# Fewer word conversions per expert, and another order of the early rows and the second early weight piece

## The chip, the cores and the metric

The kernel runs on one core of one Trainium2 chip. The metric is the device time of one execution in microseconds (us); the time of a kernel is the median of its runs. Matrix products run on TensorE (PE in the profile, its weight loads PEld), elementwise work on VectorE (DVE) and ScalarE (ACT), conversions' additions and all gathers on GpSimd (POOL), most loads are issued by SyncE (SP).

## What is computed

Three stages, one after the other. Inputs and output are float32, but for the last stage's weights: they come as float64, and the chip makes float32 of their high and low words.

```python
# 1: linear attention, 4 x 8 heads, 768 steps, head size 48
for t in range(S):
    state = alpha[:, :, t, :, None] * state + einsum('bhd,bhe->bhde', k[:, :, t], v[:, :, t])
    y[:, :, t] = einsum('bhd,bhde->bhe', q[:, :, t], state)
# 2: mixture of 8 experts over 3072 rows of 384, one expert a row (argmax of the gate's logits)
for e in range(E):
    mask = e_idx == e
    h = np.maximum(x[mask] @ w1[e], 0.0)            # 384 -> 1024
    out[mask] = gate_w[mask, None] * eom[mask, e, None] * (h @ w2[e])   # 1024 -> 384
# 3: a = x @ w1; b = x @ w2; h = a * b @ w3; return h @ w_out
```

## The kernel before

Every large product is made of three TensorE matmuls (`mm3`, lines 168 to 171): each operand is kept as a high part (rounded) and a low part (the rest), and high x high, high x low and low x high are added up in one PSUM bank.

**Attention** goes over 24 blocks of 128 rows (loop over j from line 554). In a step, TensorE makes block j's output (`a_y`), the small gate product of block j + 1 (`a_vw`), the transposed keys (`a_tk`), and the score products of block j + 2 (`a_pt`), which VectorE and ScalarE mask in the next step (`a_mask`). VectorE's queue begins a step with that mask, so what stands behind it (logits, routing, splits) waits when the score products are late. In the last steps the first expert is prepared: the most frequent expert so far is chosen, its first 256 rows are gathered (`k_rows`, two gathers of 128), and `k_turn` (steps 21 and 22) transposes them on TensorE once they have landed; `k_split` makes their low part.

**The first expert** starts with those 256 rows: `k_up(q)` (line 617) multiplies weight piece q of four (two of the eight 128-wide output blocks each) in 18 matmuls of 256 columns. The order written out is: `k_up(0)`, the end of the routing, the gather of the other 208 rows, the feeding of pieces 1 to 3, `k_up(1)`, `early_h(0)`, `k_up(2)`, `early_h(1)`, the transposes of the other rows (`x_turn`), `k_up(3)`, the splits of those rows, then eight passes of nine matmuls over the other rows in three PSUM banks in turn. A piece is fed (`feed`, line 151) by a ScalarE copy that rounds it to the high part and a VectorE difference that gives the low part. The next experts' gathers (`x_gather`) are issued on GpSimd as soon as the row numbers are there.

**Experts** follow one after the other: eight steps of the first projection (`e_up`), eight of the second (`e_down`). Between the steps stand feeds of coming pieces and, from expert 2 on, single steps of a generator (`conv`): the conversion of the last stage's weights. A conversion (`words` and `m_convert`) has four steps: ScalarE's absolute value of the high words (line 132); three VectorE operations (134 to 136); nothing; ScalarE's copy of the low words (139), the load of the next but one (953), GpSimd's addition (141) and a store to DRAM (957). There are 23; three empty steps come first. Its two buffers mean that the first step of conversion c waits for the store of conversion c - 2. All of it stands in the engines' queues between the experts' own evictions (`h_split`: ScalarE's relu and VectorE's low part).

In experts 2, 3 and 4 a step of the generator follows each of the 16 steps, so four conversions an expert; in 5 and 6 one follows each second step of the first projection and every step of the second, so three. After expert 6, `w_prime` multiplies the last two weight matrices (eight blocks f of eight g), with three steps in each block, at g = 1, 4, 7. Expert 7 has none; its second projection is done in three parts d of eight, and each part is stored and split for the last stage.

**Loads.** SyncE loads units of two pieces, 768 KB (`load_ahead`, line 108), in a fixed order: experts 0 to 6 (units 0 to 27), the converted pieces of the first eight units (28 to 35), expert 7 (36 to 39), the other converted pieces (40 to 43). Up to four units are loaded ahead between units 6 and 41, else two. A converted unit must have been stored before its load is issued.

**The last stage** goes over six groups of 512 rows: eight steps of two products (pab) and an elementwise product, then four output tiles of 24 matmuls (o).

Of the kernel before, what the change touches and what calls it, by code (L numbers as in the profile page):

```python
# [23 lines left out]
E = 8  # L24
F = 1024
KF = F // 128
# [30 lines left out]
def attention_then_moe_kernel(ctx, tc, pk0, pka, pkb, wbd_d, wexp, wmlp, cst_d, out):  # L57
# [41 lines left out]
    units = [u for e in range(E - 1) for u in sunits(e)] + runits(0, N_WO + N_W3)  # L99
    units += sunits(E - 1) + runits(N_WO + N_W3, N_D)  # L100
    Y_FIRST, Y_END = 6, len(units) - (N_M + 1) // 2
    assert Y_END % 4 == 0
    stream = [(u, c, key) for u, un in enumerate(units) for c, key in enumerate(un[2])]
    wmlp_w = wmlp.bitcast(I32)
# [1 line left out]
    loaded, freed, fed, pools = [0], [0], [0], {}  # L106

    def load_ahead():
        while loaded[0] < min(freed[0] + (4 if Y_FIRST <= loaded[0] < Y_END + 2 else pools["keep"]), pools["upto"]):
            kind, i, parts = units[loaded[0]]  # L110
            slot = loaded[0] % 4
            if Y_FIRST <= loaded[0] < Y_END and slot > 1:
                raw = ys_p.tile([128, 2 * NPC], I32, tag=f"y{slot - 2}", name="raw")
            else:
                raw = pools["raw"].tile([128, 2 * NPC], I32, tag=pools["tag"], name="raw")
            if 2 <= loaded[0] < 4:
                G.memset(raw[:, 0:1], 0)
            if kind == "r":
                for h in range(len(parts)):
                    SP.dma_start(out=raw.bitcast(F32)[:, h * NPC:(h + 1) * NPC], in_=wm_d[i + h])  # L120
            else:
                SP.dma_start(out=raw.bitcast(F32),
                             in_=wexp[bass.ds(first[i // 4] + i % 4, 1)].rearrange("o p n -> p (o n)"))
            raws[loaded[0]] = raw
            loaded[0] += 1
# [67 lines left out]
    def tiles(n):  # L193
        return [(i, min(128, n - 128 * i)) for i in range((n + 127) // 128)]
# [360 lines left out]
    for j in range(NJ):  # L555
# [47 lines left out]
            A.activation(out=early[4], in_=ps_c[:, 1, :], func=ACTF.Copy)  # L603
        if j == JK + 3:
            k_load()
        if NJ - 3 <= j < NJ - 1:
            k_turn(j - NJ + 3)
        a_pt(j + 2)
        a_dv(j)
        a_next(j - 2)  # L610
        a_alpha(j + 4)
# [2 lines left out]
    ps_k = atp.enter_context(tc.tile_pool(name="ps_k", bufs=4, space=PSUM, reuse_waits="tile"))  # L614
    uk = {}

    def k_up(q):
        w = pieces["e", 0, q]
        uk[q] = ps_k.tile([128, 2, NK], F32, tag="k", name="uk")
        for f in range(2):  # L620
            for k in range(KD):
                sl = slice((f * KD + k) * 128, (f * KD + k + 1) * 128)
                mm3(uk[q][:, f], w[:, 0, sl], w[:, 1, sl], xt[0][:, 0, k, 0:NK], xt[0][:, 1, k, 0:NK], k == 0, k == KD - 1)

    r_expert(*R_LAST)
    r_sort(JK, R_LAST[0])
# [234 lines left out]
            h_tile(2 * q + f)  # L861
            h_split(2 * q + f, uk[q][:, f], 0, NK)

    k_up(1)
    early_h(0)
    k_up(2)
    early_h(1)
    for i, n in tiles(width(0))[2:]:
        for d in range(KD):
            x_turn(bank[d], xg[0], d, i, n, NK)  # L870
    k_up(3)
    for d in range(KD):
        x_split(0, d, xg[0], bank[d])
    interleave(picks())
# [161 lines left out]
    def w_prime():  # L1036
        wpr = wpr_p.tile([128, KF, DM], F32, tag="wpr", name="wpr")
        for f in range(KF):
            ps = ps_u.tile([128, CMX], F32, tag="u", name="u")[:, 0:DM]
            for g in range(KF):  # L1040
# [9 lines left out]
                if f == KF - 1 and g % 2:  # L1050
                    pieces.pop(("o", g // 2))
                    feed(1)
                if g in (1, 4, 7):
                    next(conv, None)
            A.activation(out=wpr[:, f], in_=ps, func=ACTF.Copy)
        pieces.pop(("3", N_W3 - 1))
# [15 lines left out]
    for e in range(E):  # L1072
        if e == 1:
            interleave(windows())
        for f in range(KF if e else 0):
            e_up(e, f, pieces["e", e, f // 2])
            if f % 2:
                pieces.pop(("e", e, f // 2))
            if (f % 2 if e < E - 1 else 3 <= f < 7):
                feed(1)  # L1080
            if e < 5 or e < E - 1 and f % 2 == 0:
                next(conv, None)
        if e == E - 1:
            col = off_of(e)
            for d in range(KD):
                feed((2, 2, 0)[d])
                for f in range(KF):
                    e_down(e, f, pieces["e", e, 4 + f // 2], [d])
                e_store(e, col, [d])
                y_split(0, [d])  # L1090
            for f in range(4):
                pieces.pop(("e", e, 4 + f))
            break
# [163 lines left out]
```

## Time and profile before

| what | us |
|---|---|
| median of 3 timed runs (lowest, highest) | 715.21 (714.85, 718.95) |
| profiled execution, device time | 710.39 |
| its span, first to last instruction | 708.4 |
| TensorE busy in the span | 670.9 |
| TensorE's mean granted clock, share of full | 0.988 |

The span is what the trace covers; the device time has 2 us more around it. By TensorE's matmuls the stages lie as follows: attention to 128.3, the first rows of expert 0 to 139.6, its other rows to 149.6, its second projection from 153.1, expert 1 to 203, experts 2 to 6 to 342, the product of the last weights to 375.4, expert 7 to 401.7, the last stage to 698. In the rows below, "idle before" in square brackets is the time in which the engine stood idle before the instruction, with what ended it; x is a count.

### The profile page before, as it was taken

Reading aid. Unit: us, or ns where it says so; the run is one execution under the profiler, and the core shown is the slowest. Engines: PE = TensorE matmul, PEld = TensorE weight load, DVE = VectorE, ACT = ScalarE, POOL = GpSimd, SP = SyncE. Lnnn points to the kernel's source line nnn. Section 1 sums busy time; section 2 is a strip of 40 time slices with the busy share of each in tenths; the row PEclk is TensorE's granted clock in tenths of the full one; section 3 lists DMA queues with packets and bytes.
Section 4 is the critical chain, followed back from the end, with each engine's and each line's share of the span. In section 5 each row is a group of like instructions: output and inputs, shape, how many; then the busy total and the mean of one; then the engine's idle time right before and its main releaser. Section 6 shows DMA issues by size and latency. Waiting matters only on the chain.

```text
span 708.4 us, 14637 instructions
## 1 busy us (share of the span) xinstructions
PE 670.9 (95%) x5904; PEld 608.3 (86%) x5904; DVE 400.2 (56%) x746; ACT 340.0 (48%) x676; POOL 204.7 (29%) x231
## 2 busy tenths in 40 slices
PE   6999998879999999999999999999999999999993
PEld 3878877769999999999998989989889889889893
DVE  7989998856948899877667464132131230330320
ACT  4787777434446767666656453232232232232220
POOL 2977776230223554452351000101101002001001
PEclk9999999989999999999999999999999999999998
DMA  9999986345267899887894200000000001001000
GB/s 290 244 278 252 248 258 219 132 133 223 90 187 261 312 331 330 298 293 283 282 317 164 90 0 12 34 0 24 23 0 34 12 0 45 1 0 45 1 11 33
DMA packets 28326, 102.53 MB, mean 145 GB/s; under 512 B 4736, under 2 KB 5120, under 8 KB 28256
## 3 DMA queue, kind: packets, MB, share of 16 engines
q1 hardware_dynamic: 21360, 77.26, 33.9%
q0 software_dynamic: 6752, 24.12, 9.8%
q8 instruction: 47, 0.77, 0.5%
q14 instruction: 23, 0.19, 0.1%
q10 hardware_dynamic: 144, 0.20, 0.1%
HBM read 83.07 MB, written 18.48 MB: 143 GB/s over the span
## 4 chain that ended last, share of the span: by engine, by line
PE 60%; DMA 4%; DVE 2%; ACT 2%; issue 1%; POOL 0%; POOLq 0%; ACTq 0%; SPq 0%; DVEq 0%
PE pab L170 9%; PE pab L169 9%; PE pab L171 9%; PE o L170 5%; PE o L169 5%; PE o L171 5%; PE u L169 3%; PE u L170 3%; PE u L171 3%; PE d L170 3%; PE d L169 3%; PE d L171 3%; DMA mraw<-in_wmlp_dram 2%; DMA wm_d<-cva 2%; DVE w L160 1%
## 5 line engine op out<-in xcount | busy, mean ns | idle before, releaser
L1150 DVE TENSOR_TENSOR p_s<-pab,a_s 128x512 f32<-128x512 f32 x48 | 33.2, 692 | 162.7 <-PE pab L171 160.4
L170 PE MATMUL pab<-y,w 128*128 128x512 f32 x288 | 112.0, 389 | 0.0
L169 PE MATMUL pab<-y,w 128*128 128x512 f32 x288 | 112.0, 389 | 0.0
L171 PE MATMUL pab<-y,w 128*128 128x512 f32 x288 | 112.0, 389 | 0.0
L1164 POOL DMA_INDIRECT out_dram<-o_s,idx_o x24 | 23.4, 975 | 296.1 <-ACT o_s L1163 291.7
L160 DVE TENSOR_TENSOR w<-raw,w 128x768 fp32r<-128x768 f32 x87 | 98.5, 1140 | 16.1 <-ACT w L159 14.4
L1152 ACT ACTIVATE ab<-p_s 128x512 fp32r<-128x512 f32 x48 | 30.3, 632 | 102.0 <-DVE p_s L1150 102.0
L159 ACT ACTIVATE w<-raw 128x768 fp32r<-128x768 f32 x87 | 71.9, 840 | 12.9 <-PE d L171 9.5
L169 PE MATMUL d<-h,w 128*128 128x464 f32 (+7 forms) x192 | 69.1, 360 | 3.1 <-ACT w L159 3.1
L141 POOL TENSOR_TENSOR cva<-cva,cvc 128x768 int32<-128x768 int32 x23 | 46.5, 2023 | 85.9 <-ACT cvc L139 70.0
L171 PE MATMUL d<-h,w 128*128 128x464 f32 (+7 forms) x192 | 67.2, 350 | 0.0
L170 PE MATMUL d<-h,w 128*128 128x464 f32 (+7 forms) x192 | 67.1, 350 | 0.0
L169 PE MATMUL o<-wpp,ab 128*128 128x384 f32 x192 | 64.2, 334 | 0.0
L171 PE MATMUL o<-wpp,ab 128*128 128x384 f32 x192 | 64.2, 334 | 0.0
L170 PE MATMUL o<-wpp,ab 128*128 128x384 f32 x192 | 64.2, 334 | 0.0
L171 PEld LDWEIGHTS pab<-y,w 128*128 128x128 f32 x288 | 54.1, 188 | 11.2
L169 PEld LDWEIGHTS pab<-y,w 128*128 128x128 f32 x288 | 54.1, 188 | 11.0
L170 PEld LDWEIGHTS pab<-y,w 128*128 128x128 f32 x288 | 54.1, 188 | 11.0
L169 PE MATMUL u<-xt,w 128*128 128x448 f32 (+6 forms) x168 | 58.5, 348 | 1.8 <-DVE h L851 1.4
L171 PE MATMUL u<-xt,w 128*128 128x448 f32 (+6 forms) x168 | 57.8, 344 | 1.4 <-DVE w L160 1.4
L170 PE MATMUL u<-xt,w 128*128 128x448 f32 (+6 forms) x168 | 57.9, 345 | 0.0
L1153 DVE TENSOR_TENSOR ab<-p_s,ab 128x512 fp32r<-128x512 f32 x48 | 33.2, 692 | 33.5 <-ACT ab L1152 33.5
(243 smaller groups left out, 1479.9 us busy)
## 6 DMA issues: line engine op xcount, KB each, us to landing
raw<-in_wexp_dram SPq DMA_DIRECT2D x32, 768.0 KB, 5.5
mraw<-in_wmlp_dram SPq DMA_DIRECT2D x23, 768.0 KB, 6.2
pb<-in_pkb_dram SPq DMA_DIRECT2D x24, 384.0 KB, 4.8
wm_d<-cva POOLq DMA_DIRECT2D x23, 384.0 KB, 3.7
raw<-wm_d SPq DMA_DIRECT2D x23, 384.0 KB, 4.7
pa<-in_pka_dram SPq DMA_DIRECT2D x42, 192.0 KB, 5.0
x_d<-xs POOLq DMA_DIRECT2D x23, 192.0 KB, 6.4
pa<-in_pka_dram SPq DMA_DIRECT2D x42, 97.5 KB, 5.4
```

Source lines behind the costliest of these rows:

```text
L141: G.tensor_tensor(out=a, in0=a, in1=c, op=ALU.add)
L159: A.activation(out=hl[:, 0], in_=src, func=ACTF.Copy)
L160: low = lambda: eng.tensor_tensor(out=hl[:, 1], in0=src, in1=hl[:, 0], op=ALU.subtract)
L169: T.matmul(out=ps, lhsT=sh, rhs=mh, start=start, stop=False)
L170: T.matmul(out=ps, lhsT=sh, rhs=ml, start=False, stop=False)
L171: T.matmul(out=ps, lhsT=sl, rhs=mh, start=False, stop=stop)
L1150: V.tensor_tensor(out=p_s, in0=pss[1], in1=a_s, op=ALU.mult)
L1152: A.activation(out=t[:, 0], in_=p_s, func=ACTF.Copy)
L1153: V.tensor_tensor(out=t[:, 1], in0=p_s, in1=t[:, 0], op=ALU.subtract)
L1164: G.indirect_dma_start(out=out[:, :], out_offset=bass.IndirectOffsetOnAxis(ap=idx_o[:, n:n + 1], axis=0), in_=o, in_offset=None)
```

## The change

In `load_ahead`, units 32 to 35 (converted pieces) come two ahead in place of four. In the attention loop, `a_pt(j + 2)` stands ahead of `k_turn`. `k_up` can do half a piece (`fs`) and can put all six matmuls with the low weights behind the twelve with the high ones (`low_last`); piece 1 is done so, and piece 3 is halved around the transposes of the other rows. In `w_prime` the first three blocks have four steps of the generator (odd g), the others three, the last none. In the experts, a step follows each second step of the first projection from expert 2 on, expert 7 too; expert 7's second projection has a step after each second f (until the conversions are through), and its feeds of the last stage's pieces are two, none, two in place of two, two, none.

```diff
+    N_LATE = Y_END - 8
...
-        while loaded[0] < min(freed[0] + (4 if Y_FIRST <= loaded[0] < Y_END + 2 else pools["keep"]), pools["upto"]):
+        while loaded[0] < min(freed[0] + (4 if Y_FIRST <= loaded[0] < N_LATE or Y_END - 4 <= loaded[0] < Y_END + 2 else pools["keep"]), pools["upto"]):
...
+        a_pt(j + 2)
         if NJ - 3 <= j < NJ - 1:
             k_turn(j - NJ + 3)
-        a_pt(j + 2)
...
-    def k_up(q):
+    def k_up(q, fs=range(2), low_last=False):
         w = pieces["e", 0, q]
-        uk[q] = ps_k.tile([128, 2, NK], F32, tag="k", name="uk")
-        for f in range(2):
-            for k in range(KD):
-                sl = slice((f * KD + k) * 128, (f * KD + k + 1) * 128)
-                mm3(uk[q][:, f], w[:, 0, sl], w[:, 1, sl], xt[0][:, 0, k, 0:NK], xt[0][:, 1, k, 0:NK], k == 0, k == KD - 1)
+        if fs[0] == 0:
+            uk[q] = ps_k.tile([128, 2, NK], F32, tag="k", name="uk")
+        blocks = [(f, k, slice((f * KD + k) * 128, (f * KD + k + 1) * 128)) for f in fs for k in range(KD)]
+        for part in ((0, 1), (2,)) if low_last else ((0, 1, 2),):
+            for f, k, sl in blocks:
+                for i in part:
+                    T.matmul(out=uk[q][:, f], lhsT=w[:, i // 2, sl], rhs=xt[0][:, i % 2, k, 0:NK],
+                             start=k == 0 and i == 0 and not (low_last and f),
+                             stop=k == KD - 1 and i == 2 and (f == 1 or not low_last))
...
-    k_up(1)
+    k_up(1, low_last=True)
     early_h(0)
     k_up(2)
     early_h(1)
+    k_up(3, [0])
     for i, n in tiles(width(0))[2:]:
         for d in range(KD):
             x_turn(bank[d], xg[0], d, i, n, NK)
-    k_up(3)
+    k_up(3, [1])
...
-                if g in (1, 4, 7):
+                if g % 2 if f < 3 else f < KF - 1 and g in (1, 4, 7):
                     next(conv, None)
...
-            if e < 5 or e < E - 1 and f % 2 == 0:
+            if e < 2 or f % 2 == 0:
                 next(conv, None)
...
-                feed((2, 2, 0)[d])
+                feed((2, 0, 2)[d])
                 for f in range(KF):
                     e_down(e, f, pieces["e", e, 4 + f // 2], [d])
+                    if f % 2:
+                        next(conv, None)
```

## Rows read from the trace of the kernel before

**Rows 1.** Page, span and busy time of TensorE.
```profile
span 708.4 us, 14637 instructions
...
PE 670.9 (95%) x5904; PEld 608.3 (86%) x5904; DVE 400.2 (56%) x746; ACT 340.0 (48%) x676; POOL 204.7 (29%) x231
```

**Rows 2.** Stages: stretch, length; busy PE, PEld, DVE, ACT, POOL; PEclk, DMA share, GB/s.
```profile
139.60:153.10 13.50, 8.77 (x75) 8.34 (x73) 5.39 (x21) 3.72 (x11) 7.61 (x8) 0.86 0.51 152
...
207.60:342.00 134.40, 133.21 (x754) 130.51 (x753) 112.80 (x148) 89.82 (x143) 57.63 (x47) 1.00 0.86 299
342.00:375.40 33.40, 33.40 (x194) 33.20 (x193) 20.27 (x25) 20.86 (x31) 15.11 (x12) 1.00 0.85 295
375.40:401.70 26.30, 24.57 (x147) 23.95 (x147) 18.60 (x24) 15.28 (x26) 2.64 (x2) 1.00 0.39 135
401.70:698.00 296.30, 295.70 (x1440) 261.73 (x1438) 83.73 (x124) 87.64 (x149) 22.42 (x23) 1.00 0.04 16
```

**Rows 3.** Waits of TensorE and its weight loads: us in total, times, longest.
```profile
PE u L171 <- DVE w L160: 1.4, 1, 1.4
PE u L169 <- DVE h L851: 1.4, 3, 0.5
...
PE uk L171 <- DVE w L160: 1.1, 1, 1.1
...
PE ps_c L479 <- DMA xg<-x_d,idx_c: 0.9, 1, 0.9
...
PEld ones L828 <- DMA xg<-x_d,idx_c: 0.3, 1, 0.3
```

**Rows 4.** Timeline of the attention's end: start, length, instruction, idle before and releaser.
```profile
121.80 0.69 DVE L337 TENSOR_TENSOR px<-pts,cm 128x512 f32<-128x512 f32 x1 [1.22 <-PE pts L331]
...
124.33 0.43 ACT L427 ACTIVATE rhs<-ohh,cst 128x160 bf16<-128x160 bf16 x1 [0.55 <-DVE ohh L425]
...
124.97 0.44 PE L365 MATMUL y<-U,q 64*64 64x64 f32 x13 [0.85 <-ACT pb L321]
```

**Rows 5.** Timeline of the early pieces, 131 to 140.
```profile
131.58 2.68 DVE L160 TENSOR_TENSOR w<-raw,w 128x768 fp32r<-128x768 f32 x3
132.58 0.38 PE L171 MATMUL uk<-xt,w 128*128 128x256 f32 x1 [1.07 <-DVE w L160]
...
139.64 0.26 PE L169 MATMUL ones<-xt,w 128*128 128x208 f32 x1
```

**Rows 6.** Timeline of expert 0's other rows and the gathers, 140 to 154.
```profile
140.53 0.97 POOL L201 DMA_INDIRECT xg<-x_d,idx_c  x1 [5.33 <-DVE idx_c L753]
...
149.33 0.95 POOL L201 DMA_INDIRECT xg<-x_d,idx_c  x1 [0.30 <-issue]
...
147.68 0.34 ACT L850 ACTIVATE h<-ps_c 128x208 fp32r<-128x208 f32 x1 [3.25 <-PE ones L171]
151.93 0.34 ACT L850 ACTIVATE h<-pts 128x208 fp32r<-128x208 f32 x1 [3.90 <-remote]
...
153.06 0.75 PE L169 MATMUL d<-h,w 128*128 128x464 f32 x1 [3.06 <-ACT w L159]
```

**Rows 7.** Conversions, 207 to 380: groups by line (busy, mean ns, idle before); DMA issues.
```profile
L141 POOL TENSOR_TENSOR cva<-cva,cvc 128x768 int32<-128x768 int32 x23 | 46.5, 2023 | 85.9 <-ACT cvc L139 70.0 <-ACT w L159 10.8 <-ACT cva L132 4.0
...
L132 ACT ACTIVATE cva<-mraw 128x768 f32<-128x768 f32 x23 | 20.8, 905 | 20.6 <-DMA wm_d<-cva 15.0 <-DMA mraw<-in_wmlp_dram 5.7
...
mraw<-in_wmlp_dram SPq DMA_DIRECT2D x23, 768.0 KB, 6.2
...
wm_d<-cva POOLq DMA_DIRECT2D x23, 384.0 KB, 3.7
```

**Rows 8.** Chain that ended last, 360 to 385: start, length, what.
```profile
364.05 0.86 ACT w L159
...
366.24 7.01 DMA wm_d<-cva
...
376.32 5.21 DVE w L160 x4
```

## Prediction: what bounds the kernel, what each edit costs, and how the numbers follow

> **What bounds the kernel now.** I read the page's busy shares first. TensorE is busy for 670.9 of 708.4 us [rows 1]. So the span can only shrink where TensorE stands idle, and the table by stage says where that is: 4.7 us between 139.6 and 153.1 (13.50 less 8.77), 1.2 us in all of 207.6 to 342 (experts 2 to 6), nothing while the two last weight matrices are multiplied (342 to 375.4), 1.7 us in expert 7, 0.6 us in the whole final part [rows 2]. The list of what TensorE waited for names the culprits: 1.1 us on the low half of an early weight piece (uk), 0.9 us on gathered rows (ps_c), 1.4 us on a low half of expert 7's first piece (u, L171), and three waits of up to 0.5 us on VectorE's h [rows 3]. Each edit of the change aims at one of these. Together the waits that it touches are under 6 us, 0.8% of the span, so a large move is not to be had from them; the question is how much of each is really given back.
>
> The sum is made against the profiled execution, 710.39 us with a span of 708.4. The median of the timed runs, 715.21, is 4.8 us longer, and no view shows where; I carry differences over to the median unchanged.
>
> **Early rows (a_pt ahead of k_turn).** Only j = 21 is affected: at j = 22 there is no block 24. TensorE waited 0.9 us for the gather before the turn [rows 3] with block 23's score products queued behind it, and VectorE's mask of block 23 stood idle 1.22 us for those, to 121.80 [rows 4]. Put first, the products fill that wait. The mask can then start when VectorE is done with the low half of piece 0, in the queue ahead of it, so VectorE gains up to 1.2 us. The gain must get through ScalarE, which works in order: the only wait that it has on that path is 0.55 us at the sorting operand (L427), and the last block's y starts, at 124.97, on the ScalarE copy that is next in its queue [rows 4]. Beyond 0.55 us ScalarE is bound by its own work. I take 0.55 us; the bounds are 0 (the score bank of block 22 still being read) and 1.2. The turn itself is not later: the rows land when they did.
>
> **Second early piece (low_last) and the split of the fourth.** The low halves of pieces 1 to 3 come from one run of three VectorE operations from 131.58, 2.68 us long, so the first ends near 132.5; TensorE's third matmul waited 1.07 us for it [rows 5]. From 132.58 to 139.64 lie 52 matmuls and six small turns in 7.06 us, so at most 0.13 us each. Twelve high products ahead of the six low ones are some 1.4 us of work, enough to cover 1.07: that wait goes. What is late next is the turn of the second rows: its weight load already waited 0.3 us for their gather [rows 3]. Nine matmuls of piece 3, 1.1 us, now stand ahead of the turn, just what was saved. So the turn stays bound by its gather, and the nine behind it (1.1 us in place of 2.2) must now cover the copies and differences of the turned rows; if they don't, up to 1.1 us of wait comes back there. Expert 0's remaining rows then start up to 1.6 us earlier (0.55 + 1.07).
>
> I count none of the 1.07, because of what follows. ScalarE's h for that pass stood idle 3.25 us to 147.68 and 3.90 us to 151.93, though the matmuls that it reads had long been issued; the copy of the next piece is behind it on ScalarE, and TensorE's down projection started at 153.06 after 3.06 us of waiting for that copy [rows 6]. Meanwhile GpSimd issued eight gathers back to back, the first at 140.53, the last at 149.33 [rows 6]. The wait ends as the gathers end. The gathers start from indices that VectorE works out after the turned rows are split, so they move by the 0.55 us of the attention tail and not by the 1.07. Value taken: 0; bounds 0 and 1.07. The Trainium skill (Perfetto Trace Analysis, section "Tensor Engine Instruction (MATMUL, LD_WEIGHTS)") says that a matmul's end in the profile is estimated from its size, and not observed. By that rule the matmuls could have been slow themselves, the stage would go at TensorE's own pace, and the 1.07 would be kept; the idle ScalarE beside matmuls at an even pitch cannot tell the two apart, so it is a rival below.
>
> **Three conversions in place of four.** A conversion is two ScalarE operations (0.905 us the first), three on VectorE, one GpSimd addition, a store of 384 KB that lands in 3.7 us, and the load of the next but one, 768 KB in 6.2 us [rows 7]. None is added or removed: 23 before and after. By the yields, experts 2, 3 and 4 now make three each; experts 5 and 6 had three already. The product of the last two matrices takes six as before, its first three blocks at four steps each and its last block none; the last two and a half go to expert 7. The first operation of conversion c waits for the store of c - 2: 15.0 of its 20.6 us of waiting, the rest is on the load [rows 7]. It stands in ScalarE's queue ahead of h, and so two of the three waits of up to 0.5 us on h come at the starts of experts 5 and 6 [rows 3]. There the rate was already three, and the place of the waiting operation (last step of the down projection, five steps behind the store it needs) is unchanged; only traffic from experts 2 to 4 is lighter. Of 1.2 us idle in that stage [rows 2] I credit 0.5; bounds 0 and 1.2.
>
> **The end of the product and the start of expert 7.** Before, a store took 7.01 us (366.24 to 373.25); the conversion behind it ran on ScalarE right after, its three VectorE operations came before the four low halves of expert 7, which therefore ran from 376.32 [rows 8]. That cost 1.4 us on the low half and 0.3 on h [rows 3]. After, the three VectorE operations stand behind those halves (first step of expert 7), but the waiting operation is still there: conversion 20 needs the store of 18, which ends in block 5, behind the copy of the last matrix piece at 364.05 [rows 8]. From there: copy 0.86, the conversion's own copy of the same width 0.9, addition 2.0 [rows 7] and 0.4 to issue give a store from about 368.2. At 3.7 us it lands at 371.9, the low half is ready before TensorE wants it, and 1.8 us are gained. At 7.01 us it lands at 375.2; 0.9 for the operation, 0.45 for the 384-wide eviction queued behind (an estimate: half of the 768-wide copy), 0.86 and 0.9 for the two halves [rows 5, 8] bring the low half to 378.3, against 377.2 before (376.32 and 0.9), and as fewer VectorE operations follow, 0.6 us are lost in all. The traffic beside it (two or three loads of 768 KB within 4 us) is that of the slow row; I take 6.2 us and a gain of 0.2. Bounds -0.6 and 1.8.
>
> **Edits at nothing.** Four units of loads come two ahead in place of four: the first weights of expert 7 are asked for in block 2 and read in block 7, 19 us later at 4.18 us a block (33.4 / 8 [rows 2]), against loads of 6 us. The last conversions in expert 7 lie under engines busy 18.6 (VectorE) and 15.3 (ScalarE) of 26.3 us [rows 2]. Their last stored pieces are ready some 18 us after the second third of the down projection (0.9 + 2.0 + 0.6 + 7.0 + 6.2 + two halves); they are read in step 6 of the final part, some 27 us after (240 matmuls take 49.4 us a group, 18 a step). Nine microseconds of cover; were it gone, each microsecond would show.
>
> **Sum.** 0.55 + 0 + 0.5 + 0.2 = 1.25 us: 710.39 to 709.1, and 715.21 to 713.9.
>
> **The rivals.**
> *The early gain is kept, or the hold at the gathers shrinks.* For it: ScalarE's idle time does not tell a late matmul from a late signal, and the gathers start elsewhere among TensorE's steps. Against it: the wait ends with the gathers. Time: 1.07 more, 712.9; if the hold's 4.7 us go as well, 708.2.
> *Slower: the store of conversion 18.* Place: ScalarE's queue ahead of expert 7's first copy. It decides once that store takes over about 7.5 us: then its loss eats the 1.05 us of the other two gains, microsecond for microsecond. A load of 768 KB in the same queues is in flight with it; at 9 us the time is 716.8.
> *Nothing comes of it.* ScalarE's order in the tail gives nothing back and the experts' waits stay: 715.2.
>
> **How the numbers follow.** The forecast, a gain of 0 to 2.5 us (711 to 715), has 0.45; the first rival 0.2 (0.06 of it with the hold gone), the slower one 0.15, no change 0.2. The range reaches down past the hold's case and up past the late store, with the runs' own spread of 714.85 to 718.95: 707.5 to 717.5. One per cent, 7.2 us, is about what a measurement of this kernel can tell from no change. Faster by more needs the hold gone and all else well: 0.08. Slower by more needs a new wait of over 7 us, which no row offers: 0.04. Within: 0.88.
>
> **What would show it.** Right: VectorE's mask of block 23 near 120.6; no uk wait; y of the last block near 124.4; ScalarE still idle in the pass beside the gathers, and the down projection at about 152.5; ScalarE's first conversion step at the end of the product still waiting for a store. Wrong: the down projection at 151.5 or earlier; expert 7 starting without a wait at all; a wait in steps 4 to 7 of the first final group, where the late pieces are read.

## The result, and the profile after

The changed kernel is slower: 724.98 us (median; 722.04 to 726.75) beside 716.19 us (714.85 to 718.95) for the kernel before, measured beside it. The ratio is 1.0128 with an interval of 1.0097 to 1.016, or 9.2 us (the medians are 8.8 us apart). The forecast was 713.9 us in a range that ended at 717.5. In the changed kernel's lines the helpers stand one further down (L170 to L172 are the three matmuls, L160 the copy of a weight piece on ScalarE, L161 its low half on VectorE, L133 the first step of a conversion, L140 its copy, L142 GpSimd's addition, L963 its store).

The page of the changed kernel, span and busy time of TensorE, to lay beside [rows 1]:

```profile
span 722.7 us, 14634 instructions
...
PE 677.0 (94%) x5904; PEld 614.4 (85%) x5904; DVE 403.5 (56%) x746; ACT 338.7 (47%) x676; POOL 204.5 (28%) x231
```

The span is 14.3 us longer than in the profiled execution before and TensorE is busy 6.1 us longer with the same 5904 matmuls; so about 8 us are idle and 6 are matmuls that took longer, with a mean granted clock of 0.976 in place of 0.988. (The profiled execution before, 710.39 us, was quicker than every timed run beside it; that is why 14.3 and 8.8 us differ.)

The table by stage of the changed kernel, beside [rows 2]; the columns are the stretch, its length, busy time of TensorE, its weight loads, VectorE, ScalarE and GpSimd, the granted clock of TensorE, the DMA engines' share and GB/s. The rows are the pass beside the gathers, the start of the down projection, experts 2 to 6, the last product in three parts, expert 7, and the final part:

```profile
138.90:153.40 14.50, 9.51 (x75) 9.05 (x73) 6.21 (x26) 3.80 (x12) 7.59 (x8) 0.85 0.55 169
153.40:160.00 6.60, 6.59 (x18) 5.34 (x19) 5.41 (x11) 2.99 (x6) 0.00 (x0) 0.56 0.36 119
205.00:341.70 136.70, 136.41 (x774) 134.82 (x775) 107.12 (x140) 86.61 (x139) 51.72 (x45) 1.00 0.77 266
341.70:354.30 12.60, 12.60 (x75) 12.60 (x74) 6.86 (x9) 7.21 (x11) 5.57 (x5) 1.00 0.93 313
354.30:366.80 12.50, 12.50 (x74) 12.50 (x73) 8.16 (x9) 6.87 (x10) 4.92 (x5) 1.00 0.60 213
366.80:388.40 21.60, 10.42 (x49) 9.17 (x47) 7.63 (x10) 7.73 (x12) 8.04 (x6) 0.83 0.83 313
388.40:415.50 27.10, 27.06 (x145) 26.57 (x146) 23.56 (x30) 18.07 (x30) 6.94 (x5) 0.88 0.43 146
415.50:711.70 296.20, 296.06 (x1440) 261.80 (x1438) 86.06 (x126) 87.11 (x148) 23.56 (x25) 1.00 0.06 20
```

Six of the eight blocks of the last product run at full pace, as before. The last two took 8.4 us before [rows 2] and take 21.6 us here: 11.2 us idle, and the clock at 0.83. Expert 7 follows at 0.88. Experts 2 to 6 have become shorter: 136.7 us with 0.3 idle, against 138.55 before.

What TensorE waited for from 128 to 430 us (us in total, times, longest), beside [rows 3]:

```profile
PE u L170 <- ACT w L160: 11.2, 2, 6.8
PE d L170 <- ACT w L160: 2.6, 1, 2.6
...
PE ones L833 <- DMA xg<-x_d,idx_c: 0.3, 1, 0.3
```

The waits on the low half of the early piece (1.1 us) and on the low half of expert 7's first piece (1.4 us) are gone. A new one stands in their place, eight to ten times as large as either: ScalarE's copy of a weight piece comes late twice. The timeline of TensorE shows where (start, length, instruction, idle time before and what ended it):

```profile
374.47 0.69 PE L170 MATMUL u<-w,w 128*128 128x384 f32 x1 [4.40 <-ACT w L160]
...
388.41 0.67 PE L170 MATMUL u<-xt,w 128*128 128x360 f32 x1 [6.80 <-ACT w L160]
```

ScalarE's timeline says why the copies were late:

```profile
356.47 0.89 ACT L133 ACTIVATE cva<-mraw 128x768 f32<-128x768 f32 x1 [4.51 <-DMA wm_d<-cva]
...
372.79 0.89 ACT L133 ACTIVATE cva<-mraw 128x768 f32<-128x768 f32 x1 [7.37 <-DMA wm_d<-cva]
373.58 0.83 ACT L160 ACTIVATE w<-raw 128x768 fp32r<-128x768 f32 x1
...
386.36 0.89 ACT L133 ACTIVATE cva<-mraw 128x768 f32<-128x768 f32 x1 [5.36 <-DMA wm_d<-cva]
...
387.52 3.04 ACT L160 ACTIVATE w<-raw 128x768 fp32r<-128x768 f32 x4
```

The three shown are the first steps of conversions 16, 18 and 20. Each waits for the store of the conversion two before it, because the sum has two buffers. While it waits, ScalarE stands still, and the copies that TensorE needs are queued right behind: one at 373.58, four at 387.52. GpSimd's timeline has the stores of 14, 16 and 18:

```profile
348.92 0.56 POOL L963 DMA_DIRECT2D wm_d<-cva  x1 [0.30 <-POOL cva L142]
...
364.38 0.84 POOL L963 DMA_DIRECT2D wm_d<-cva  x1 [0.30 <-POOL cva L142]
...
380.34 0.84 POOL L963 DMA_DIRECT2D wm_d<-cva  x1 [0.30 <-POOL cva L142]
```

From store to the first step that it releases: 348.92 to 356.47, 364.38 to 372.79, 380.34 to 386.36, so 7.5, 8.4 and 6.0 us. From that first step to its own store: 356.47 to 364.38 and 372.79 to 380.34, so 7.9 and 7.5 us. Going round once through a buffer takes 13.6 to 16.3 us, and two conversions must fit into it. The schedule asks for two in 8.4 us in the first three blocks (four steps a block) and for two in 11.1 us after that. The trip is longer than either, so the chain 14, 16, 18, 20 waits at every link (4.5, 7.4 and 5.4 us), and its last two waits stand in front of copies that TensorE needs at once.

The sum of the waits on that operation makes the same point. ScalarE from 335 to 400 us, before:

```profile
ACT cva L132 <- DMA wm_d<-cva: 7.4, 4, 4.8
```

and after:

```profile
ACT cva L133 <- DMA wm_d<-cva: 19.7, 4, 7.4
```

### The profile page after: what moved, and what is told of

It is laid out like the page before. It is cut to its first block, busy times and chain, and to the rows that moved or that the text cites. A ratio compares the mean times of both kernels' runs of the same rounds, so it can differ in the third digit from the quotient of the medians.

```text
span 722.7 us, 14634 instructions
## 1 busy us (share of the span) xinstructions
PE 677.0 (94%) x5904; PEld 614.4 (85%) x5904; DVE 403.5 (56%) x746; ACT 338.7 (47%) x676; POOL 204.5 (28%) x231
## 5 line engine op out<-in xcount | busy, mean ns | idle before, releaser
L161 DVE TENSOR_TENSOR w<-raw,w 128x768 fp32r<-128x768 f32 x87 | 95.2, 1102 | 32.2 <-ACT w L160 29.9
L170 PE MATMUL pab<-y,w 128*128 128x512 f32 x288 | 112.0, 389 | 0.0
L172 PE MATMUL pab<-y,w 128*128 128x512 f32 x288 | 112.0, 389 | 0.0
L142 POOL TENSOR_TENSOR cva<-cva,cvc 128x768 int32<-128x768 int32 x23 | 45.6, 1984 | 121.6 <-ACT cvc L140 95.6
L160 ACT ACTIVATE w<-raw 128x768 fp32r<-128x768 f32 x87 | 71.3, 838 | 9.9 <-PE d L172 9.5
L170 PE MATMUL d<-h,w 128*128 128x464 f32 (+7 forms) x192 | 69.6, 362 | 2.6 <-ACT w L160 2.6
L172 PE MATMUL d<-h,w 128*128 128x464 f32 (+7 forms) x192 | 67.7, 352 | 0.0
L170 PE MATMUL u<-xt,w 128*128 128x448 f32 (+6 forms) x168 | 59.3, 353 | 7.3 <-ACT w L160 6.8
L170 PE MATMUL o<-wpp,ab 128*128 128x384 f32 x192 | 64.2, 334 | 0.0
L172 PE MATMUL o<-wpp,ab 128*128 128x384 f32 x192 | 64.2, 334 | 0.0
L171 PEld LDWEIGHTS pab<-y,w 128*128 128x128 f32 x288 | 54.1, 188 | 11.5 <-DVE y L952 0.6
L172 PEld LDWEIGHTS pab<-y,w 128*128 128x128 f32 x288 | 54.1, 188 | 11.2
L170 PEld LDWEIGHTS pab<-y,w 128*128 128x128 f32 x288 | 54.1, 188 | 11.0
L171 PE MATMUL u<-xt,w 128*128 128x448 f32 (+6 forms) x168 | 59.0, 351 | 0.0
L172 PE MATMUL u<-xt,w 128*128 128x448 f32 (+6 forms) x168 | 58.9, 351 | 0.0
```

What stands on the lines that cost most here:

```text
L142: G.tensor_tensor(out=a, in0=a, in1=c, op=ALU.add)
L160: A.activation(out=hl[:, 0], in_=src, func=ACTF.Copy)
L161: low = lambda: eng.tensor_tensor(out=hl[:, 1], in0=src, in1=hl[:, 0], op=ALU.subtract)
L170: T.matmul(out=ps, lhsT=sh, rhs=mh, start=start, stop=False)
L171: T.matmul(out=ps, lhsT=sh, rhs=ml, start=False, stop=False)
L172: T.matmul(out=ps, lhsT=sl, rhs=mh, start=False, stop=stop)
```

## The experiments

All ratios are to the kernel before, timed beside the run on the same chip. Four chips took part; the kernel before took 707.4 us on the first (e1 to e4), 716.1 on the second (e5 to e8), 716.8 on the third (e9 to e12) and 706.6 on the fourth (e13 to e15). Gains and losses in us go by the ratio unless medians are named; the two can differ by up to 3 us. Stages are compared by the first matmul of each in the timeline of TensorE, "last product" up to expert 7's first matmul.

The theories. **Density**: four steps a block go round the two buffers faster than a store allows. **Loads**: holding units 32 to 35 to two ahead puts loads and stores into one clump. Both would act through one place, ScalarE's first step of a conversion waiting ahead of weight copies. The **rival** is that engines or DMA are simply overloaded in that stretch, wherever the wait stands.

**The early part alone, the conversions alone.** The first kernel has only the edits to a_pt, low_last and the halved k_up(3); the second only the others:

```
e1:  a_pt(j + 2) first;  k_up(1, low_last=True);  k_up(3, [0]) ... k_up(3, [1])
e2:  - if g in (1, 4, 7):
     + if g % 2 if f < 3 else f < KF - 1 and g in (1, 4, 7):
     - if e < 5 or e < E - 1 and f % 2 == 0:
     + if e < 2 or f % 2 == 0:
     + two loads ahead for units N_LATE to Y_END - 5; feed((2, 0, 2)[d]); steps in e7's down
```

> Only the early part of the change: the score products ahead of the turn, the low matmuls of the second piece last, the fourth piece in halves; the conversions and the loads as before. Theory A (all of the loss lies in the conversions at the end of the product of the last weights): the median is that of the kernel before within 2 us, at best 1 us less; the wait of 1.1 us on uk is gone, expert 0's second projection still starts with the end of the gathers. Rival B (the early part costs something later, by the half clock that TensorE had for 6 us in the second projection of expert 0): 1.5 to 3 us more than before.

> Only the conversions and the order of loads of the change, the early part as before. Theory A: all of the change's loss, 8 to 10 us over the kernel before, with ScalarE's first conversion step waiting 4 to 8 us for a store twice or more in the product of the last weights and TensorE idle 10 us or more there. Rival B: 6 to 7 us over, the rest being the early part's.

Measured: e1 705.56 us, ratio 0.9968 (0.9942 to 0.9995), a gain of 2.3 us; e2 718.49 us, ratio 1.0163 (1.0126 to 1.0201), a loss of 11.5 us. The waits of e2, of TensorE from 150 to 430 us and of ScalarE from 335 to 400:

```profile
PE u L170 <- ACT w L160: 9.2, 2, 6.2
```
```profile
ACT cva L133 <- DMA wm_d<-cva: 19.2, 5, 7.5
```

The whole loss is in the conversions, at the same two places as in the full change. It is a little more than the 8 to 10 us expected. The early part gains more than the 1 us that was expected at best, and more than the 0.55 us of the prediction.

**Density and loads, each undone.** e3 is e2 with steps at g in (1, 4, 7) in all eight blocks; e4 is e2 with units 32 to 35 three ahead in place of two:

```
e3:  + if g in (1, 4, 7):
e4:  + 3 if N_LATE <= loaded[0] < Y_END - 4 else ...
```

> As the conversions alone (e2), but with three steps in each of the eight blocks of the product of the last weights, as before, in place of four in the first three and none in the last; the same 24 steps. Theory A1 (a conversion with two buffers takes 6 to 7 us around, and the first three blocks ask for one each 4.2 us): about half of the loss goes, 3 to 6 us over before. Rival A2 (the loads of expert 7's first weights, issued in one go, lengthen the stores): the loss stays at 8 to 10 us.

> As the conversions alone (e2), but units 32 to 35 are loaded three ahead in place of two: the loads of the last converted unit and of expert 7's first two no longer come in one go, but one in block 1 and one in block 2 of the product. Rival A2: the stores take 4 to 6 us in place of 6 to 8 and the time is 0 to 4 us over before. Theory A1: no more than 2 us are gained, 6 to 9 us over before.

Measured: e3 710.59 us, ratio 1.0032 (1.0008 to 1.0055); e4 713.89 us, ratio 1.0098 (1.0065 to 1.0132). The last product took 45.2 us in e2, 36.5 in e3 and 41.6 in e4. What TensorE waited for in e3:

```profile
PE u L170 <- ACT w L160: 3.0, 1, 3.0
PE u L172 <- DVE w L161: 1.4, 1, 1.4
```

and in e4:

```profile
PE u L170 <- ACT w L160: 7.0, 1, 7.0
```

Undoing the density gave back 7.9 of the 11.1 us between the medians, undoing the load order 4.6. e3 did better than its theory (3 to 6 us over; it is 2.3 over). e4 is 6.9 us over, in the range of the density theory, but gained more than the 2 us which that theory allowed it. The two gains sum to 12.5 us, more than the whole; whether they are independent the next two runs were to tell.

**Both undone, without and with the early part.** e5 is e2 with the edits of e3 and e4; e6 is the full change with them:

> Conversions moved as in the change, but with three steps in every block of the last product and with units 32 to 35 loaded three ahead; early part as before. Two causes that add (density of the steps, late loads), both acting through the same operation of ScalarE that waits for a store: 11.1 less 7.9 less 4.6, about 1.4 us under the kernel before, and the two waits on ScalarE's copies of weight pieces in the last product are gone or under 3 us together. One cause seen twice (a chain of stores that either mending breaks): it stays where even steps alone stood, 2 to 4 us over the kernel before, with expert 7's first piece still 3 to 5 us late.

> The whole change with both mendings of the run before it. If the early part and the conversions do not touch each other: 1.8 us under that run, so about 3 us under the kernel before if the causes add, about 1 us over it if they do not.

Measured: e5 717.58 us, ratio 1.0 (0.9974 to 1.0027); e6 713.29 us, ratio 0.9944 (0.9917 to 0.9971), 4.0 us faster than the kernel before. The last product of e5 took 37.4 us, no less than e3's 36.5; ScalarE's waits on the first step in e5 (330 to 405 us):

```profile
ACT cva L133 <- DMA wm_d<-cva: 8.0, 3, 5.8
ACT cva L133 <- DMA mraw<-in_wmlp_dram: 6.9, 2, 6.1
```

In the stage the two causes do not add: with even steps, the earlier loads bring nothing more to the product, and the wait has partly gone over to the load of the conversion's words. The time is less clear: e5's interval runs from 1.9 us under the kernel before to 1.9 over, between the two readings (1.4 under, 2 to 4 over) and on another chip than e3. So that one cause was seen twice is what the last product shows, from one execution of each; it is not shown by the times. e6 is the first version of the change that beats the kernel before, by 4.0 us where 3 was the better of its two expectations. That does not decide it either: of the 4.9 us between the profiled executions of e5 and e6, the pass beside the gathers has 3.5 (24.73 and 21.19 us), the stretch behind it 1.8 and the last product 1.1, while e6's attention took 3.0 us longer.

**The wait put three steps later.** e7 is e2, e8 the early part alone, each with the buffers exchanged: one for the first step's result, two for the sum.

```
- for t, n in (("a", 2), ("c", 1))          + for t, n in (("a", 1), ("c", 2))
- G.tensor_tensor(out=a, in0=a, in1=c, ...) + G.tensor_tensor(out=c, in0=a, in1=c, ...)
```

> Conversions and loads exactly as in the change (four steps a block, two loads ahead), early part as before; only which of a conversion's two tiles has two buffers is exchanged, and GpSimd adds into the other one. The wait for the store before last then stands in front of the conversion's fourth step on ScalarE in place of its first, three steps (3 to 4 us) later; stores, loads and their traffic stay. Theory of the place in ScalarE's queue: the four waits of 2.4, 4.5, 7.4 and 5.4 us shrink by 3 to 4 us each, TensorE's waits on the copies of weight pieces fall from 17 to under 6 us, and the time from 11 us over the kernel before to 0 to 5 us over it. Rival, that the traffic itself (loads and stores in one clump) slows the weights' own loads: the time stays within 2 us of 11 over, with TensorE waiting for loads in place of ScalarE.

> The change's early part, the conversions at their places of before, with the exchanged buffers of the run before this one. If the place of the wait on ScalarE already cost something in the kernel before (its own waits at that operation in the last product were 0.9, 0.9 and 4.8 us, and expert 7's first low half was 1.4 us late): 1 to 2 us under the early part alone, so 2.5 to 4 us under the kernel before. If those waits were hidden: the same as the early part alone, 1.8 us under.

Measured: e7 726.09 us, ratio 1.0101 (1.0069 to 1.0133); e8 716.56 us, ratio 1.0002 (0.9977 to 1.0027). Both expectations of the theory failed: e7 is 7.2 us over the kernel before by the ratio and 10.0 by the medians, not 0 to 5, and e8 lost the early part's gain. ScalarE's waits in e7, and TensorE's:

```profile
ACT cva L133 <- POOL cvc L142: 14.7, 5, 4.1
ACT cva L133 <- DMA mraw<-in_wmlp_dram: 6.5, 1, 6.5
```
```profile
PE u L170 <- ACT w L160: 9.5, 1, 9.5
```

The wait for the store is gone (0.3 us is left at L140), but with a single buffer for the first step's result, that step now waits for GpSimd's addition of the conversion before it, and stands in the same place. So this edit exchanged one wait for another in front of the same copies. It does not separate the theory from the rival, which had TensorE waiting for loads.

**The store taken out of the cycle.** In e9 (e2 otherwise) each store takes its bytes from a constant tile, so no buffer waits for it. In e10 (e2), e11 (the full change) and e12 (the early part alone) the sum has three buffers; the room comes from shifting the low words in place.

```
e9:        - G.dma_start(out=wm_d[i], in_=a)   + G.dma_start(out=wm_d[i], in_=cst[:, 0:NPC])
e10-e12:   + a = pools["cv"].tile(..., bufs=3)
           - A.activation(out=c, in_=lw.bitcast(U32), ...); read(); G.tensor_tensor(a, a, c)
           + A.activation(out=lw, in_=lw.bitcast(U32), ...); G.tensor_tensor(a, a, lw); read()
```

> Conversions and loads exactly as in the change, early part as before, but each converted piece's store takes its 384 KB from the constant tile in place of the sum, so nothing waits for a store to leave the conversion's buffer; queue, bytes and time of issue stay, and the loads of the stored pieces still wait for their stores. Left out: the converted words never reach the later products. Theory (ScalarE's first step of a conversion stands in its queue in front of copies of weight pieces and waits for the store before last): the 19 us of that wait are gone, the product of the last two matrices takes 33 to 35 us in place of 45, expert 7's first piece is under 2 us late, and the time falls from 11 us over the kernel before to within 2 us of it. Rival (the clump of stores and loads itself is what is slow, or three conversions in 12.5 us are too much for ScalarE, VectorE and GpSimd): still 7 to 11 us over, with the waits on loads or on the conversion's own steps.

> Conversions and loads exactly as in the change, early part as before, with a third buffer for the conversion's sum; the room comes from writing the shifted low words in place over the loaded words, so the load of the next but one is asked for after the addition, some 2.4 us later. The first step of a conversion then waits for the store three before, not two. Theory: the waits for stores (2.4, 4.5, 7.4, 5.4 us) shrink by one period of 4 us or more each and nearly vanish; what may come in their place is the load, late by 2.4 us. The last product at 34 to 38 us, time 0 to 4 us over the kernel before. Rival as in the run before: still 7 to 11 us over.

> The whole change with the third buffer of the run before it: that run's time less the early part's 1.8 us, so 2 us under to 2 us over the kernel before by the theory, 5 to 9 us over by the rival.

> The change's early part alone, conversions at their places of before, with the third buffer. In the kernel before the first step of a conversion waited 15.0 us for stores in all. If some of it reached TensorE (0.9 to 1.4 us at expert 7's first piece, waits on h in experts 2 to 6): 1 to 3 us under the early part alone, 3 to 5 us under the kernel before. If it was all hidden: 1.8 us under the kernel before, as the early part alone.

| run | us, median | ratio to before | last product, us |
|---|---|---|---|
| e9, store from a constant | 718.61 | 1.0015 (0.9992 to 1.0038) | 38.7 |
| e10, third buffer | 723.06 | 1.0079 (1.0055 to 1.0102) | 42.0 |
| e11, full change, third buffer | 720.24 | 1.0044 (1.0019 to 1.007) | 42.0 |
| e12, early part, third buffer | 713.15 | 0.9928 (0.9897 to 0.9959) | 33.3 |

e9 says how much hangs on the wait for the store. With the same stores in the same queue, the loss falls from 11.5 us in e2 to 1.1, and the last product from 45.2 to 38.7 us, where the kernel before takes 33.3 to 33.8. (e2 was timed on another chip; each loss is against the kernel before on its own chip.) So the wait for the buffer, and not the traffic, cost most of the time and over half of what the product lost; the rival is out as the main cause. It is not out altogether, for 38.7 us is more than the 33 to 35 of the expectation, and TensorE's wait of 5.3 us more than its 2. ScalarE's first step in e9, and below it TensorE:

```profile
ACT cva L133 <- DMA mraw<-in_wmlp_dram: 16.0, 5, 5.7
```
```profile
PE u L170 <- ACT w L160: 5.3, 1, 5.3
```

The step now waits for its own words: the loads have two buffers as well and are asked for by the conversion two before. How much of the 5 us left comes from this second pair of buffers, and how much from slower traffic, no run tells. In e10 this wait grew, as the load is asked for behind the addition, and 5.7 us of loss remained, between the 0 to 4 of the theory and the 7 to 11 of the rival:

```profile
ACT cva L133 <- DMA mraw<-in_wmlp_dram: 19.1, 6, 4.9
```
```profile
PE u L170 <- ACT w L160: 8.5, 1, 8.5
```

e11 lies 2.5 us under e10, the early part once more; at 3.2 us over the kernel before it falls between its two expectations. With the conversions at their places of before, e12 gains 5.2 us on the kernel before, the best ratio of all and the upper end of what was expected if the waits had reached TensorE; there the later load did no harm (33.3 us for the last product, 25.3 in place of 26.2 for expert 7).

**All mendings together, and both kernels once more on one chip.** e13 is e6 with the third buffer, e14 the kernel before, e15 the changed kernel.

> The whole change with all three mendings: three steps in every block of the last product, units 32 to 35 three ahead, a third buffer for the sum. If the 11 us of waiting for stores that the two mendings left on ScalarE (its longest, 5.2 us, in front of expert 7's first copies) still cost TensorE something, 2 to 3 us under the version without the third buffer, so 6 to 7 us under the kernel before. If the load, now asked for 2.4 us later, takes the place of the store, no better than the third buffer with the early part alone: 4 to 5 us under.

> The kernel before once more, for its stages on this chip. If the hold at the gathers belongs to the chip and not to the kernel: the time from the first early product to the down projection is that of the two runs beside it within 1 us (the early part's own gain). If what experts 2 to 6 gained (1.9 us between the two profiles, in place of 0.5) is larger in an ordinary execution: 140 to 143 us here against 137 in the run of the change.

> The changed kernel once more, on the same chip as the two beside it. If its 8.8 us came from the conversions and not from the hold at the gathers or from chance: 7 to 11 us over the kernel before, the last product at 43 to 47 us with two waits of TensorE for ScalarE's copies, experts 2 to 6 at 136.5 to 137 us. If a share of it was the hold: 3 to 6 us over.

Measured: e13 710.0 us, ratio 1.0028 (1.0002 to 1.0055); e15 717.16 us, ratio 1.0143 (1.0093 to 1.0194); one execution of e14, 709.5 us. e13 fell short of both of its expectations: 2.0 us slower than the kernel before, with the load in the store's place. Its expectations went by e6 and e12, which ran on chips where the kernel before is 10 us slower; neither was run on this one. e14 and e15 came out as expected (the pass at the gathers within 1 us of each other, experts 2 to 6 at 141.5 and 136.6 us, the changed kernel 10.1 us over with its last product at 45.5).

```profile
ACT cva L133 <- DMA mraw<-in_wmlp_dram: 17.4, 6, 6.5
```

The stages of e14 and e15, first matmul to first matmul, us:

| stage | e14, before | e15, changed | difference | forecast |
|---|---|---|---|---|
| first early product to the down projection | 19.42 | 18.60 | -0.82 | 0 |
| down projection of expert 0, expert 1 | 48.80 | 48.82 | 0.0 | 0 |
| experts 2 to 6 | 141.46 | 136.62 | -4.84 | -0.5 |
| last product | 33.81 | 45.54 | +11.73 | -0.2 (with expert 7's start) |
| expert 7 | 26.20 | 26.42 | +0.2 | 0 |
| final part | 295.86 | 296.29 | +0.4 | 0 |

The differences sum to +6.7 us; the attention ahead of the table was 0.9 us shorter in e15 (forecast 0.55). The medians are 10.6 us apart; the execution of e14 was 3 us above its kernel's median and that of e15 1.6 us below, so the profile pair shows less than the runs do. Where the rest of it lies no view shows; experts 2 to 6 of the kernel before are one place that varies (138.55 us in the first profile, 141.46 here).

Experts 2 to 6 of e14 and of e15, table by stage:

```profile
199.20:340.60 141.40, 137.93 (x774) 134.35 (x775) 112.94 (x149) 90.47 (x145) 60.04 (x51) 1.00 0.85 293
```
```profile
197.40:334.10 136.70, 136.42 (x775) 134.84 (x776) 107.15 (x140) 86.53 (x139) 51.82 (x45) 1.00 0.77 265
```

and what ScalarE's first step waited for there in e14 (199 to 341 us); in e15 the operation is not in that list at all:

```profile
ACT cva L132 <- DMA wm_d<-cva: 8.3, 5, 2.9
ACT cva L132 <- DMA mraw<-in_wmlp_dram: 5.9, 2, 3.9
```

So the change did empty experts 2 to 6 of these waits: 14.2 us on ScalarE, and 3.2 us of idle TensorE. The other 1.5 us are matmuls that were busy for less time at the same granted clock (137.93 and 136.42 us); why stays open. What was taken out here came back in the last product, where weight copies stand directly behind the waiting step.

## Why the prediction was wrong, step by step

**The step that failed** is the sentence that the product of the last two matrices "takes six as before, its first three blocks at four steps each and its last block none". The number of conversions is the same, and that was all the forecast priced. The pitch is not: in the first three blocks it is two conversions in 8.4 us in place of 11.1. The rows for the check were there. From a conversion's first step to its store are three steps and copy, addition and issue, 0.9 + 2.0 + 0.4 us [rows 7]; at four steps a block of 4.18 us that is 3.1 + 3.3 = 6.4 us, and with a store of 3.7 to 7.0 us [rows 7, 8] 10.1 to 13.4 us round the buffer, against 8.4 allowed. So a link in those blocks lacks 1.7 to 5 us. At the old pitch it is 4.2 + 3.3 + 3.7 = 11.2 us against 11.1, so by the median store the old schedule just fitted. Measured were 13.6 to 16.3 us round after the change, and 11.2 us of waiting in TensorE; undoing the pitch alone (e3) gave back 7.9 us, taking the store out of the trip (e9) all but 1.1.

The pitch is not the whole of it. The kernel before was late by its own measure: the first steps of its conversions 17 to 22 start at 342.95, 348.09, 353.12, 359.54, 365.81 and 373.27, so its last trips took 10.2, 11.5, 12.7 and 13.7 us. Its longest wait already stood ahead of expert 7's first copies:

```profile
373.27 0.89 ACT L132 ACTIVATE cva<-mraw 128x768 f32<-128x768 f32 x1 [4.82 <-DMA wm_d<-cva]
374.07 0.47 ACT L1055 ACTIVATE wpr<-u 128x384 f32<-128x384 f32 x1
374.45 1.57 ACT L159 ACTIVATE w<-raw 128x768 fp32r<-128x768 f32 x2
```

It ended just in time there: TensorE lost no more than the 1.4 us on the low half and 0.3 on h [rows 3]. In e3, at the old pitch, ScalarE still waited 15.5 us for stores from 330 to 405 us, and TensorE 3.0 for a copy.

**The store's price.** The sum used 3.7 to 7.0 us for a store, from the median and from the one long row. That median stands on few stores: in that trace four of the 23 show a landing. In e14, the same kernel, all 23 do, and took 2.9 us at least, 4.7 in the median and 8.0 at most. After the change a store took 6.0 to 8.4 us until the first step that it released. The Trainium skill (DMA: Bandwidth & Descriptors, section "Anatomy of one DMA — SWDGE (gpsimd) path") gives a fit of about 2.0 us plus the bytes at 436 GB/s for one such transfer, an estimate of 2.9 us for these 384 KB. The quickest store of each of the two profiles of the kernel before agrees with that, at 2.9 us; the median of 4.7 us and the 6.0 to 8.4 us of the chain do not, and the measurement decides.

**Loads two ahead, costed at nothing.** The forecast looked only at when expert 7's weights were needed, with 19 us of cover. What it missed is the store beside them: undoing this edit alone gave 4.6 us (e4). With even steps it brought nothing more to the product (e5), so it looks like part of the same chain and not like a term of its own; that rests on one execution of each.

**The end of the product and expert 7's start.** The slower rival named the place rightly, ScalarE's queue ahead of expert 7's first copy and the store of conversion 18, and worked out that 9 us of store would give 716.8. (The load beside that store goes through SyncE's queue and the store through GpSimd's [rows 7], not through the same one.) But it let that store start at 368.2; it started at 380.34, 12 us later, as the links before it had slid. The size was off because one link was priced and not the chain. "Slower by more needs a new wait of over 7 us, which no row offers" was wrong twice. The range ends 3.6 us above the forecast, so a wait of that length was enough. And the operation with 15.0 us of such waits in the kernel before [rows 7] offered it.

**Experts 2 to 6.** The direction and the mechanism were right; the size of 0.5 us, with 1.2 as its bound, was not. It was 1.9 us between the first two profiles and 4.8 us between e14 and e15. The bound came from the idle time in one execution that happened to be a good one: experts 2 to 6 took 138.55 us in it and 141.46 in e14.

**The attention's end** was right in its mechanism. VectorE's mask of block 23 waited 1.22 us before [rows 4] and 0.31 after:

```profile
121.66 0.69 DVE L338 TENSOR_TENSOR px<-pts,cm 128x512 f32<-128x512 f32 x1 [0.31 <-PE pts L332]
```

The block before it was masked 0.77 us later in this execution than in the one before (117.66 for 116.89), and yet the first early product started only 0.26 us later (128.58 for 128.32): 0.5 us gained, 0.55 forecast. ScalarE's wait of 0.55 us at the sorting operand [rows 4] is gone as well. The size rests on this pair, and on e14 and e15 with 0.9 us; over all runs the first early product starts anywhere from 128.3 to 132.9 us.

**The second early piece** was forecast at nothing because of the hold at the gathers. In the changed kernel's profile it came so: the wait of 1.07 us is gone, and the pass to the down projection took 24.83 us in place of 24.74. Gathers and ScalarE of that execution, beside [rows 6]:

```profile
140.81 0.97 POOL L202 DMA_INDIRECT xg<-x_d,idx_c  x1 [5.32 <-DVE idx_c L758]
...
149.59 0.95 POOL L202 DMA_INDIRECT xg<-x_d,idx_c  x1 [0.30 <-issue]
...
147.98 0.34 ACT L855 ACTIVATE h<-ps_c 128x208 fp32r<-128x208 f32 x1 [4.00 <-remote]
152.29 0.34 ACT L855 ACTIVATE h<-pts 128x208 fp32r<-128x208 f32 x1 [3.96 <-PE ps_c L172]
```

That agreement is in part luck. On the chips with the hold, this pass took 24.8, 24.1, 24.1, 21.9 and 21.2 us with the early part (the changed kernel, e11, e12, e8, e6) and 24.7, 24.7, 24.7, 24.9 and 25.8 without (the kernel before, e5, e7, e10, e9). The early part was worth 2.5 us from e10 to e11 and 4.0 from e5 to e6, where the prediction had 0.55. So the hold was often shorter with it, as the first rival had it; why stays open.

In the changed kernel's profile TensorE, which had idled 2.45 us to 148.79 and 2.56 us to 153.41, was also longer at the lower of its two clock levels (1.2 and 2.4 GHz): 0.56 granted from 153.4 to 160, against 0.78 from 153.1 to 160 in the kernel before. From the down projection to expert 2 it took 51.6 us in place of 50.4.

**The last conversions in expert 7's down projection** were forecast at nothing and cost little: 0.2 us in expert 7 and 0.4 in the final part of e15, with no wait of TensorE there. Where the 0.4 comes from was not followed up.

## What to carry to other kernels

A step that is moved must be priced by its pitch as well as by its number: add up one trip round its buffers, transfer included, and compare it with the time that the schedule allows for as many steps as there are buffers. If the trip is longer, the lateness adds up link by link and comes out wherever an in-order engine has work queued behind the waiting instruction. And a wait that is taken from a stretch where it was half hidden has gone somewhere: look for what stands behind it there before counting the gain; here the early part with a third buffer (e12) kept its gain, and so did the change with even steps and earlier loads (e6), each on one chip where the kernel before takes 716 to 717 us. On a chip where it takes 707, e6's version with a third buffer (e13) was 2.0 us slower than the kernel before.

## What the runs showed of the hardware

The hold beside the back-to-back gathers goes with the chip first of all. From the first early product to the down projection, executions on two chips took 18.6 to 19.5 us (e1 to e4 and e13 to e15, the kernel before and the changed one among them); e5 to e12 on two other chips took 21.2 to 25.8 us with the same gathers, and the first two profiles 24.7 and 24.8. ScalarE on a chip without the hold (e1), beside gathers issued from 141.12 to 150.90 us:

```profile
144.68 0.34 ACT L854 ACTIVATE h<-ps_c 128x208 fp32r<-128x208 f32 x1 [0.66 <-PE ps_c L171]
145.69 0.35 ACT L854 ACTIVATE h<-pts 128x208 fp32r<-128x208 f32 x1 [0.66 <-PE pts L171]
```

The waits of 3 to 4 us are 0.66 us here, and the kernel before takes 707 us on these two chips and 716 to 717 on the two others. There the early part's gain is kept (19.3 to 19.5 us in e2 to e4, 18.6 in e1). The first rival of the prediction, with the hold gone, thus describes these chips, and there the kernel before has no hold either (e14). Each of the four chips was used once, so these runs do not tell the chip from the occasion. What holds ScalarE on the other chips stays open: the Trainium skill's rule that a matmul's end in the profile is estimated (Perfetto Trace Analysis, section "Tensor Engine Instruction (MATMUL, LD_WEIGHTS)") leaves a slow matmul and a late signal alike in the trace, and no run here tells them apart.
